# A pruned matmul on one core: the second token pair's load moved from ScalarE's queue to SyncE's

## The chip, the cores and the metric

One NeuronCore of a Trainium2 chip runs the whole program. The time is device microseconds of one execution. Before the change the median of 3 runs is 233.1 us (232.97 to 233.29). The profile is of one execution, which took 233.29 us.

## The reference

A weight matrix `w` (1024 x 1024) is pruned 2:4 along its rows: in each group of 4 neighbouring rows, column by column, the two entries of largest magnitude stay and the others become zero. The pruned matrix is multiplied with 8192 tokens and a bias is added. All arrays are bf16.

```python
B, S, D = 16, 512, 1024
N, M = 2, 4
G = D // M
wg = w.reshape(G, M, D)
mag = jnp.abs(wg)
order = jnp.argsort(mag, 1)
thr = jnp.take_along_axis(mag, order[:, M - N:M - N + 1, :], 1)
mask = (mag >= thr).astype(w.dtype)
wp = (wg * mask).reshape(D, D)
return jnp.einsum("bsd,df->bsf", x, wp) + b
```

## The kernel before

The 8192 tokens are 64 tiles of 128. The contraction of 1024 is 8 slices of 128 rows, and the 1024 output columns are two halves of 512, each with one PSUM bank.

The weights are loaded so that the four rows of a group lie beside each other in one partition (`w_gh`, L60 to L71), which lets VectorE find thresholds without moving data between partitions. They are cut into six pieces (L61): the first row half in four pieces of 256 columns, the second in two of 512. `abs_piece` (L109) and `prep_piece` (L124) compute magnitudes, thresholds, mask and the pruned weights of one piece. Piece 0 is pruned in parts, so that TensorE can begin before the piece is done.

TensorE must not wait for all pieces, so the first 14 tiles are computed in an order written out by hand, the string FRONT (L285 to L299). Tiles 0 to 7 use the first row half in the layout in which it was loaded. Their tokens have to be transposed and regrouped to fit it: token halves are loaded plainly (`load_x`, L76, tiles `xh`), transposed on TensorE with an identity (`transpose_half`, L177; token T of FRONT; matmuls at L182), copied from PSUM to SBUF by ScalarE (`copy_half`, L184; C; L187, tiles `xT`), and used as stationary operand of `mm_part` (L191; N and M; L203). In FRONT, `N.0.1.0` is piece 0, tile 1, row slice 0. A tile's four transposes read one `xh`; its matmuls read its `xT` and a pruned piece. W and w are matmuls of constants (L105) ahead of the first transposes.

The second row half of tiles 0 to 7 comes by a transposing DMA (`xg`, L324), tiles 8 to 13 by two more (`xfill`, L259), and both use `wp_nat`, the pruned weights in natural row order, which DMAs make from the pieces (`unpack`, L170 to L172). From tile 14 on a plain loop (L361 to L377) runs 16 matmuls for each tile on tokens from transposing DMAs (`xTs`, `xTb`, L271); VectorE adds the bias while it empties the banks (L248), and ScalarE's queue sends the outputs.

`K` (L26) keeps each engine's instructions in the order in which they are written. DMAs are issued by SyncE (SP) and ScalarE (ACT), each on a queue of its own; in the profile SP's DMAs are q1 and ScalarE's are q10. At the start, SP issues the first two of the four group rows of piece 0, then the token pair 0 and 1 (`xh_0`), tile 4 (`xh_4`), tile 5 (`xh_5`), piece 1, the pair 6 and 7 (`xh_6`), pieces 2 and 3 in one, and then FRONT's first DMAs: piece 4 and the first transposing load. ScalarE issues the other two group rows of piece 0 and the pair 2 and 3 (`xh_2`), and then loads its function table and makes its first copy (L100). DMAs signal through eight semaphores handed out in turn, so that a later DMA is issued only when the earlier one with its semaphore has landed. In the program before, the first transposing load (L259) has the semaphore that `xh_2` used.

Of the kernel before, what the change touches and what calls it, by code (L numbers as in the profile page):

```python
# [10 lines left out]
def kernel(  # L11
# [7 lines left out]
    nc = tc.nc  # L19
# [56 lines left out]
    def load_x(ta, tb, eng=nc.sync):  # L76
        xt = const.tile([P, tb - ta, KH], bf16, name=f"xh_{ta}")
        src = xf[ta * P:tb * P, 0:KH].rearrange("(t p) c -> p t c", p=P)
        K(eng.dma_start(xt[:], src))
        for t in range(ta, tb):  # L80
            xh[t] = xt[:, t - ta, :]
# [1 line left out]
    load_w(0, 0, 256, nc.sync, 0, 2)  # L83
    load_w(0, 0, 256, nc.scalar, 2, 4)
    load_x(0, 2)
    load_x(2, 4, nc.scalar)
    load_x(4, 5)
    load_x(5, 6)
    load_w(0, 256, 512)
# [316 lines left out]
```

## Time and profile before

| what | value |
|---|---|
| median of 3 runs | 233.1 us |
| profiled execution | 233.29 us |
| its span, first to last instruction | 231.5 us |
| TensorE matmuls busy | 226.3 us (98%) |
| VectorE busy | 120.2 us (52%) |
| ScalarE busy | 18.0 us (8%) |
| granted TensorE clock | 1.000 |
| HBM read, written | 3.41 MB, 16.78 MB |

"Busy" is the time in which an engine ran at least one instruction that counts; PE is TensorE's matmuls, PEld its weight loads, which overlap with matmuls, and DVE is VectorE. The chain that ended last is followed back from the last instruction, at each step to what released it. In a timeline the columns are start, duration, engine, line, operation, output and input, shapes, count, and in brackets the idle time before it and what ended it. DMA issues stand as SPq or ACTq: the duration there is the issue alone, and the landing is listed apart, as microseconds from the start of the issue. A table by stretches of time lists for each the busy time and count of PE, PEld, DVE, ACT and POOL, then the granted clock, the share of the 16 DMA engines' time, and GB/s.

### The profile page before, as it was taken

What the parts mean: (1) busy time and instruction counts of PE and PEld (TensorE: products, weight loads), DVE (VectorE), ACT (ScalarE), POOL (GpSimd) and SP (SyncE); (2) the same over time, 40 slices, a digit from 0 to 9 for tenths busy, and PEclk for the clock granted to TensorE, in tenths of its full rate; (3) what the DMA queues carried; (4) which work ended last, traced back from release to release, by engine and by line L of the source; (5) the groups of instructions that cost most, each with busy time, mean ns of one, the idle gap of its engine ahead of it and who ended that gap; (6) DMA issues with size and microseconds to landing.
All of it is one profiled execution on the core that took longest, in us unless ns stands there. A gap on an engine that the chain in (4) does not pass through costs nothing.

```text
span 231.5 us, 2773 instructions
## 1 busy us (share of the span) xinstructions
PE 226.3 (98%) x1137; PEld 110.5 (48%) x1156; DVE 120.2 (52%) x213; ACT 18.0 (8%) x33; POOL 0.7 (0%) x6
## 2 busy tenths in 40 slices
PE   7999999999999999999999999999999999999995
PEld 3887444444444444444444444444444444444443
DVE  3999887867997324424424424423423433433434
ACT  2867500000000000000000000000000000000000
POOL 1000000000000000000000000000000000000000
PEclk9999999999999999999999999999999999999999
DMA  6999889999647222991249622595128921122222
GB/s 196 295 193 270 192 177 184 267 252 307 258 181 272 91 95 65 233 290 55 84 120 265 159 95 91 131 258 179 69 91 210 316 108 40 53 91 91 91 93 91
DMA packets 77100, 38.19 MB, mean 165 GB/s; under 512 B 63136, under 2 KB 68896, under 8 KB 77088
## 3 DMA queue, kind: packets, MB, share of 16 engines
q1 hardware_dynamic: 67712, 20.91, 42.0%
q10 hardware_dynamic: 9376, 17.11, 20.0%
q8 instruction: 9, 0.15, 0.3%
q14 instruction: 3, 0.02, 0.0%
HBM read 3.41 MB, written 16.78 MB: 87 GB/s over the span
## 4 chain that ended last, share of the span: by engine, by line
PE 96%; DMA 2%; issue 1%; DVE 0%; SPq 0%
PE bank L371 73%; PE bank L203 17%; PE bank L263 6%; DMA xh<-in_x_dram 2%; PE bank L182 1%; DVE o_last L354 0%; SPq L71 0%; PE bank L105 0%
## 5 line engine op out<-in xcount | busy, mean ns | idle before, releaser
L371 PE MATMUL bank<-wp_nat,xTb 128*128 128x512 bf16 x737 | 161.7, 379 | 0.8
L248 DVE TENSOR_TENSOR o_pair<-bank,bias_sb 128x512 bf16<-128x512 f32 x104 | 67.3, 687 | 99.5 <-PE bank L371 94.2
L371 PEld LDWEIGHTS <-xTb 128*128 128x128 bf16 x752 | 73.6, 98 | 88.7
L239 DVE TENSOR_TENSOR stage<-bank,stage 128x512 f32<-128x512 f32 x22 | 14.2, 687 | 4.1 <-PE bank L203 4.1
L203 PE MATMUL bank<-w,xT 128*128 128x256 bf16 x128 | 14.7, 273 | 0.0
L243 DVE TENSOR_TENSOR o_pair<-stage,bias_sb 128x512 bf16<-128x512 f32 x22 | 14.0, 683 | 0.0
L203 PE MATMUL bank<-wp_nat,xg 128*128 128x512 bf16 x62 | 13.9, 379 | 0.1
L203 PEld LDWEIGHTS <-xT 128*128 128x128 bf16 x128 | 12.2, 98 | 1.8 <-ACT xT L187 0.3
L235 ACT COPY stage<-bank 128x512 f32<-128x512 f32 x22 | 11.5, 613 | 4.5 <-PE bank L203 4.5
L203 PE MATMUL bank<-wp_nat,xfill 128*128 128x512 bf16 x47 | 10.6, 379 | 0.1
L263 PE MATMUL bank<-wp_nat,xfill 128*128 128x512 bf16 x47 | 10.5, 379 | 0.1
L203 PEld LDWEIGHTS <-xg 128*128 128x128 bf16 x64 | 6.3, 98 | 7.6
L263 PEld LDWEIGHTS <-xfill 128*128 128x128 bf16 x48 | 4.7, 98 | 5.7
L203 PEld LDWEIGHTS <-xfill 128*128 128x128 bf16 x48 | 4.7, 98 | 5.5
L371 PE MATMUL bank<-wp_nat,xTs 128*128 128x512 bf16 x32 | 7.1, 379 | 0.0
L150 DVE TENSOR_TENSOR mask<-mag,thr 128x512 bf16<-128x512 bf16 (+3 forms) x10 | 5.6, 581 | 0.2
L153 DVE TENSOR_TENSOR w<-w,mask 128x512 bf16<-128x512 bf16 (+3 forms) x10 | 5.6, 580 | 0.1
L371 PEld LDWEIGHTS <-xTs 128*128 128x128 bf16 x32 | 3.1, 98 | 3.8
L105 PE MATMUL bank<-const-bfloat16-1.0 128*128 128x512 bf16 (+1 forms) x12 | 4.0, 493 | 0.8 <-PEq L390 0.8
L187 ACT COPY xT<-bank 128x512 bf16<-128x512 bf16 x8 | 4.1, 605 | 3.0 <-PE bank L182 3.0
L120 DVE TENSOR_SCALAR mag<-w 128x512 uint16<-128x512 uint16 (+2 forms) x6 | 2.7, 466 | 2.8 <-DMA w<-in_w_dram 2.7
L263 PE MATMUL bank<-wp_nat,xTb 128*128 128x64 bf16 (+3 forms) x40 | 3.7, 251 | 0.0
(20 smaller groups left out, 26.1 us busy)
## 6 DMA issues: line engine op xcount, KB each, us to landing
out_dram<-o_pair ACTq DMA_DIRECT2D x24, 512.0 KB, 2.8
out_dram<-o_pair ACTq DMA_DIRECT2D x15, 256.0 KB, 2.0
wp_nat<-w SPq DMA_DIRECT2D x16, 128.0 KB, 2.8
w<-in_w_dram SPq DMA_DIRECT2D x3, 512.0 KB, 5.9
xh<-in_x_dram SPq DMA_DIRECT2D x2, 256.0 KB, 4.2
xh<-in_x_dram ACTq DMA_DIRECT2D x1, 256.0 KB, 4.4
xh<-in_x_dram SPq DMA_DIRECT2D x2, 128.0 KB, 4.2
w<-in_w_dram SPq DMA_DIRECT2D x1, 256.0 KB, 4.5
```

What stands on the lines that cost most here:

```text
L105: K(nc.tensor.matmul(bank[7][:, :n], lhsT=ones[:, :P], rhs=ones[:, :n], start=True, stop=True))
L120: K(nc.vector.tensor_single_scalar(mag[:, ms].bitcast(u16), w_of(i)[:, ms].bitcast(u16), 0x7FFF, op=Alu.bitwise_and))
L150: K(nc.vector.tensor_tensor(mask[:, ms, c], mag[:, ms, c], tb, op=Alu.is_ge))
L153: K(nc.vector.tensor_tensor(w_of(i)[:, ms, c], w_of(i)[:, ms, c], mask[:, ms, c], op=Alu.mult))
L187: K(nc.scalar.copy(xt[:], src))
L203: K(nc.tensor.matmul(dst, lhsT=lhs, rhs=rhs, start=c0 == 0 and m == 0, stop=c1 == FH and m == 3))
L235: K(nc.scalar.copy(stage[(h, t)][:], bank[own[(h, t)]][:]))
L239: K(nc.vector.tensor_tensor(st, bank[own[(2 + h, t)]][:], st, op=Alu.add))
L243: K(nc.vector.tensor_tensor(get_o(t)[:, f], stage.pop((h, t))[:], bias_sb[:, f], op=Alu.add))
L248: K(nc.vector.tensor_tensor(get_o(t)[:, f], bank[bk][:], bias_sb[:, f], op=Alu.add))
L263: K(nc.tensor.matmul(bank[bk][:, :c1 - c0], lhsT=xN[t][:, kt, :], rhs=wp_nat[h][:, kt, c0:c1], start=kt == 0, stop=kt == KT - 1))
L371: K(nc.tensor.matmul(bank[bks[h]][:], lhsT=xN[t][:, kt, :], rhs=wp_nat[h][:, kt, :], start=kt == 0, stop=kt == KT - 1))
```

## The change

```diff
@@ -83,7 +83,7 @@
     load_w(0, 0, 256, nc.sync, 0, 2)
     load_w(0, 0, 256, nc.scalar, 2, 4)
     load_x(0, 2)
-    load_x(2, 4, nc.scalar)
+    load_x(2, 4)
     load_x(4, 5)
     load_x(5, 6)
     load_w(0, 256, 512)
```

`load_x` issues on SyncE where no engine is given. The load of tiles 2 and 3 is therefore issued by SP, as its third DMA, behind tiles 0 and 1 and ahead of tile 4. ScalarE is left with one load at the start, the second two group rows of piece 0. In the built program nothing else moves: TensorE's, VectorE's and GpSimd's instructions are the same, and only the two semaphores of `xh_0` and `xh_2` are exchanged, so that the first transposing load now has the semaphore that `xh_0` used.

## The prediction

> **What bounds the kernel now.** I read the page from the top: busy shares, then the chain that ended last, then the first 11 us instruction by instruction, because every DMA that the change touches is issued before 2 us.
>
> ```profile
> PE 226.3 (98%) x1137; PEld 110.5 (48%) x1156; DVE 120.2 (52%) x213; ACT 18.0 (8%) x33; POOL 0.7 (0%) x6
> ...
> PE 96%; DMA 2%; issue 1%; DVE 0%; SPq 0%
> ```
>
> TensorE is the bound and its work is not touched. The time can only change through where TensorE's stream begins and where it is held. The chain in order of time shows the only part outside TensorE:
>
> ```profile
> 0.73 0.45 SPq L71
> 1.18 0.06 issue
> 1.24 3.96 DMA xh<-in_x_dram
> 5.20 0.05 issue
> 5.24 1.08 PE bank L182 x16
> ```
>
> So the first token pair (xh_0, tokens 0 and 1) lands at 5.20 and starts the transposes T.0. The weight loads of TensorE, which lead its matmuls, show where it is held after that:
>
> ```profile
> 5.24 0.93 PEld L182 LDWEIGHTS <-xh 128*128 128x128 bf16 x16 [0.89 <-DMA xh<-in_x_dram]
> ...
> 6.39 0.15 PEld L203 LDWEIGHTS <-xT 128*128 128x128 bf16 x2
> 6.82 0.11 PEld L203 LDWEIGHTS <-xT 128*128 128x128 bf16 x2 [0.28 <-ACT xT L187]
> 6.94 0.33 PEld L182 LDWEIGHTS <-xh 128*128 128x128 bf16 x4
> 7.31 1.43 PEld L203 LDWEIGHTS <-xT 128*128 128x128 bf16 x14
> ```
>
> The reader is to see two holds. Tile 1's first matmul (6.82) waits for ScalarE's second copy, and tile 2's (7.31) comes when the third copy has ended. The copies run back to back:
>
> ```profile
> 5.69 3.04 ACT L187 COPY xT<-bank 128x512 bf16<-128x512 bf16 x6 [2.41 <-PE bank L182]
> ```
>
> Six copies in 3.04 us are one per 0.49, with 0.60 for the last one (median 597 ns). Copies 1, 2 and 3 end at about 6.28, 6.77 and 7.25; the loads that need the second and third start 0.05 later. The train starts at 5.69 because T.0 does, so both holds descend from xh_0's landing.
>
> **The size of the holds.** Taken one by one in the trace, weight loads stand 0.109 us apart behind a 256-column matmul and 0.056 behind a transpose. From the load at 6.444 the third load on stands at 6.943 and would stand at 6.771 at this spacing: 0.17 lost. From 7.164 the third stands at 7.433 instead of 7.385: 0.05 lost. Together 0.22 us.
>
> **What else is due just in time.** xh_2 (tokens 2 and 3) was issued at 1.25 and landed after 4.4, at 5.62; its first weight load is at 5.66, straight behind T.1. Tile 4 (xh_4) landed at 5.98 and T.4 starts at 6.17. VectorE's second prune of piece 0 ends at 6.36 and the first pruned matmul's load is at 6.39, its start at 6.44. These three end within 0.2 us of TensorE's need, so a later xh_2 moves 6.44 one for one, and an earlier one buys at most 0.03.
>
> **The change part by part.** *ACT queue:* one issue of 0.505 us goes. ScalarE's table load moves from 1.79 to about 1.3. ScalarE next waits for T.0 until 5.69 (2.41 idle), so this is worth 0. Without that cover it would be 0.5.
>
> *SP queue:* xh_2 goes in behind xh_0. Three x issues took 1.44, so a place in the queue is 0.48 to 0.50. Every later SP issue moves by that: xh_4 from 1.75 to 2.24, xh_5 2.25 to 2.74, w piece 1 from 2.72 to 3.2, xh_6 3.44 to 3.9, the two 512 KB w loads (4.09, 4.70) by the same, all of them one DMA each.
>
> *The queue past 5 us:* the xfill transpose starts now at 5.63, because its semaphore is that of xh_2 (5.62) while SP was free at 5.33. After, its semaphore slot belongs to xh_0 and SP is free at 5.33 + 0.49 = 5.82: it starts 0.2 later, its 6.48 us then end at 12.3, and the unpacks (12.25), the last w load (15.79) and xg (16.46) go 0.2 later. The next unpacks at 22.48 wait for VectorE's prune, so the shift ends there. Covers: the unpacked rows landed at 17.85 and are read at 21.2; the xg rows landed at 23.8 and are read at 26.3. Worth 0; uncovered it would be 0.2.
>
> *Landings:* the shift in issue matters only if the engines ran dry. They do not:
>
> ```profile
> 3.25:3.75 0.50, 0.50 (x3) 0.19 (x2) 0.17 (x1) 0.04 (x1) 0.00 (x0) 1.00 1.08 260
> 3.75:5.25 1.50, 0.78 (x6) 0.32 (x4) 1.50 (x9) 0.00 (x0) 0.00 (x0) 1.00 1.02 358
> 5.50:8.50 3.00, 3.00 (x39) 2.57 (x37) 2.81 (x11) 2.81 (x6) 0.00 (x0) 1.00 1.05 330
> ```
>
> The last two columns are DMA share and GB/s. From 3.75 to 5.25, with both rings at work, the engines are full at 358 GB/s, and the packets split 52.7% (SP's ring) to 49.5% (ACT's): the two pairs share the engines. From 5.5 to 8.5 SP's ring alone moved 330.
>
> ```profile
> q1 hardware_dynamic: 297, 0.28, 52.7%
> q10 hardware_dynamic: 271, 0.26, 49.5%
> ```
>
> In one ring xh_0 comes first. It had 0.13 MB by 3.75; the other 0.13 MB at 330 GB/s take 0.4, so its packets end near 4.15 instead of about 4.7, and it lands near 4.7 to 4.8 instead of 5.20. The 0.26 MB of xh_2 follow in 0.8: packets end near 4.95 instead of 5.25, so it lands at 5.3 to 5.6. What comes behind is bounded by the rates: 1.5 us at 330 instead of 358 leave 0.04 MB over, 0.13 us. So xh_4 lands at 5.98 to 6.11 (needed 6.17), w piece 1 at 7.25 to 7.38.
>
> *Piece 1 on VectorE:* its first operation started at 7.27, on the landing, and its first half was pruned at 10.36; TensorE reads that from 10.74. A landing at 7.38 makes it 10.49; TensorE 0.22 earlier asks at 10.52. It holds, barely. Piece 2 (half at 13.68, asked 14.24) has 0.5 to spare.
>
> *Sum:* TensorE's 6.44 stays (gain 0 to 0.03). With xh_0 at 4.78, copies 1 and 2 end at 5.87 and 6.35, before tile 1's load at 6.55; copy 3 ends near 6.84, before tile 2's at 7.22. Both holds go: 0.22. The holds at copies 7 and 8 (near 9.9 and 10.4) repeat, since T.6 and T.7 move with TensorE. The profiled execution took 233.29, of which 231.5 is span; 0.22 off gives 233.07. The median of the runs shown is 0.19 below that execution, so the forecast is 233.1 - 0.2 = 232.9. The bounds on the gain in xh_0's landing are 0 (then nothing) and 0.5; 0.26 is enough.
>
> I count 0.2% (0.47 us) as what a measurement can tell from no change, so this is a gain inside it.
>
> The Trainium skill speaks against any gain: "DMA: Bandwidth & Descriptors", "Issuing engines are not separate DMA queues", says that DMAs of both engines run on the same 16 DMA engines and that issuing on two saves only sequencer time. By that rule the change would cost one SP issue, which is the issue-bound rival below; the trace agrees with the sharing (52.7 to 49.5), and whether order within a ring is worth anything the rule leaves open.
>
> **Rivals.** *Hidden anyway* (0.10): xh_0 does not land earlier, being held by latency, not by its neighbour; xh_2 lands as before. For: 260 GB/s in 3.25 to 3.75 with the ring almost alone. Time 233.1.
>
> *Issue-bound* (0.15): landings stand 4.0 to 4.5 after their issue for all x loads and piece 1, and this may be a fixed delay. Then xh_0 stays at 5.20, xh_2 lands at 6.12, the first pruned matmul's load moves by 0.50 to 6.89; no copy is waited for any more, which gives 0.22 back; piece 1's half at 10.86 comes before TensorE's 11.02. Loss 0.28: 233.4. Against: the full engines above.
>
> *A ring has a rate of its own* (0.20), the one that ends slower: if one ring alone draws only what each drew from 3.75 to 5.25 (0.26 MB in 1.5 us, 180 GB/s), xh_0 gains nothing and xh_2 comes 1.46 after it, at 6.66, 1.04 late. Less the 0.22 that is then no longer waited for, 0.8: 233.9. It decides as soon as xh_2 lands more than 0.22 late, after 5.84, and by over 0.2% after 6.31. For: the slow half microsecond before 3.75. Against: 330 GB/s of that ring alone later.
>
> *More than the holds* (0.10): the two w halves of piece 0 (3.55 and 3.73) land 0.3 earlier too, VectorE starts so much earlier and 6.44 moves with it: 0.22 + 0.3, 232.6. Against: before 3.25 almost no x packet was moving, so there is little to take away.
>
> **How the numbers follow.** Forecast 0.45, the rivals as given. Within 0.2% (232.63 to 233.57) fall forecast, hidden and issue-bound, 0.70, less 0.02 for a forecast that spreads below and 0.03 for an issue-bound case that spreads above: 0.65. Faster is 0.10 + 0.02 = 0.12, slower 0.20 + 0.03 = 0.23. The range 232.5 to 233.9 leaves out the lower part of "more than the holds" and the upper half of the slow ring, some 0.15. The likeliest case's own range is 232.7 to 233.2.
>
> **What would show it.** Right: xh_0's weight load (L182) near 4.8, a wait inside the 16 transposes before T.2, the hold on copy 2 gone from the waits, the first pruned matmul still near 6.4, piece 1's first operation within 0.13 of 7.27, and 0.2 off the span. Wrong: T.0 still at 5.24 (hidden or issue-bound); T.2 at 6.1 (issue-bound) or beyond 6.3 (slow ring); a new wait of TensorE on VectorE near 10.5, if piece 1 is more than 0.15 late.

## The result and the profile after

The changed kernel takes 234.56 us (median of 6 runs, 234.16 to 235.49) against 233.14 before (median of 6): the ratio is 1.0065 with a 95% interval of 1.0051 to 1.0079. It is slower by 1.4 us, outside the range. The profiled execution took 234.63, its span is 232.8 against 231.5.

TensorE's weight loads of the changed kernel show where the 1.3 us of span are lost (columns as in the timeline before):

```profile
4.67 0.78 PEld L182 LDWEIGHTS <-xh 128*128 128x128 bf16 x8
6.48 0.49 PEld L182 LDWEIGHTS <-xh 128*128 128x128 bf16 x8 [1.03 <-DMA xh<-in_x_dram]
...
7.19 0.37 PEld L203 LDWEIGHTS <-xT 128*128 128x128 bf16 x4
7.58 0.33 PEld L182 LDWEIGHTS <-xh 128*128 128x128 bf16 x4
7.85 1.46 PEld L203 LDWEIGHTS <-xT 128*128 128x128 bf16 x14
10.16 0.48 PEld L182 LDWEIGHTS <-xh 128*128 128x128 bf16 x8 [0.84 <-DMA xh<-in_x_dram]
```

T.0 begins at 4.67 instead of 5.24, but T.2 waits for xh_2 until 6.48, so the first pruned matmul's load stands at 7.19 instead of 6.39: 0.80 lost. The holds on copies 2 and 3 are gone (four L203 loads in one piece, no wait inside), and with the next loads TensorE is 0.58 behind: 0.22 came back. Then T.6, which never waited before, waits for xh_6 until 10.16; its load stood at 8.74 before. From there TensorE is 1.34 late and stays so.

The transfers themselves, by stretches of time, first of the kernel before:

```profile
3.75:4.25 0.50, 0.50 (x4) 0.21 (x3) 0.50 (x4) 0.00 (x0) 0.00 (x0) 1.00 0.89 317
4.25:4.75 0.50, 0.28 (x3) 0.10 (x1) 0.50 (x4) 0.00 (x0) 0.00 (x0) 1.00 1.10 383
...
7.50:9.00 1.50, 1.50 (x17) 1.37 (x16) 1.43 (x6) 1.23 (x3) 0.00 (x0) 1.00 1.04 348
```

and of the changed one:

```profile
3.75:4.25 0.50, 0.50 (x3) 0.23 (x2) 0.50 (x4) 0.00 (x0) 0.00 (x0) 1.00 0.93 104
4.25:4.75 0.50, 0.50 (x4) 0.22 (x3) 0.50 (x3) 0.00 (x0) 0.00 (x0) 1.00 0.25 86
...
7.50:9.00 1.50, 1.50 (x19) 1.37 (x16) 0.08 (x1) 1.50 (x4) 0.00 (x0) 1.00 0.71 151
```

The last column is GB/s. Two holes have opened. After xh_0 is through, the engines move 104 and 86 GB/s where they moved 317 and 383; and from 7.5 to 9 they move 151 where they moved 348. The DMA share beside them (0.93 and 0.25) books a packet's whole time where it starts, so it does not show how full each half microsecond was.

Last landings of the first x and w loads, read from the trace's landing events (us), for the two profiled executions and three further ones:

| load | before | before, 2nd | after | after, 2nd | after, 3rd |
|---|---|---|---|---|---|
| xh_0 | 5.20 | 4.82 | 4.38 | 4.75 | 4.58 |
| xh_2 | 5.62 | 5.17 | 6.44 | 6.01 | 6.10 |
| xh_4 | 5.98 | 5.58 | 6.76 | 6.38 | 6.46 |
| piece 1 | 7.25 | 6.84 | 8.89 | 7.50 | 7.55 |
| xh_6 | 7.94 | 8.34 | 10.12 | 11.00 | 9.09 |
| time of that execution | 233.29 | 232.97 | 234.63 | 235.51 | 233.62 |

### The profile page after: what moved, and what is told of

Its sections match the earlier page's. It is cut to its first block, busy times and chain, and to the rows that moved or that the text cites. A ratio compares the mean times of both kernels' runs of the same rounds, so it can differ in the third digit from the quotient of the medians.

```text
span 232.8 us, 2792 instructions
## 1 busy us (share of the span) xinstructions
PE 227.9 (98%) x1156; PEld 110.9 (48%) x1156; DVE 120.2 (52%) x213; ACT 18.2 (8%) x33; POOL 0.7 (0%) x6
## 3 DMA queue, kind: packets, MB, share of 16 engines
HBM read 3.41 MB, written 16.78 MB: 87 GB/s over the span
## 4 chain that ended last, share of the span: by engine, by line
PE 94%; DMA 3%; SPq 1%; DVE 0%; issue 0%
PE bank L371 73%; PE bank L203 16%; PE bank L263 6%; DMA xh<-in_x_dram 3%; SPq L79 1%; SPq L71 0%; DVE o_last L354 0%; PE bank L182 0%
## 5 line engine op out<-in xcount | busy, mean ns | idle before, releaser
L248 DVE TENSOR_TENSOR o_pair<-bank,bias_sb 128x512 bf16<-128x512 f32 x104 | 67.3, 687 | 99.5 <-PE bank L371 96.3
L203 PE MATMUL bank<-w,xT 128*128 128x256 bf16 x128 | 14.5, 273 | 0.0
L203 PE MATMUL bank<-wp_nat,xg 128*128 128x512 bf16 x64 | 14.1, 379 | 0.0
L203 PEld LDWEIGHTS <-xT 128*128 128x128 bf16 x128 | 12.3, 98 | 1.6
L203 PE MATMUL bank<-wp_nat,xfill 128*128 128x512 bf16 x48 | 10.7, 379 | 0.0
L203 PEld LDWEIGHTS <-xg 128*128 128x128 bf16 x64 | 6.2, 98 | 7.6
L203 PEld LDWEIGHTS <-xfill 128*128 128x128 bf16 x48 | 4.7, 98 | 5.5
L182 PE MATMUL bank<-ident,xh 128*128 128x128 bf16 x32 | 2.8, 233 | 1.4 <-DMA xh<-in_x_dram 1.4
```

Of the source, the lines that this page charges most:

```text
L182: K(nc.tensor.transpose(dst[:, m, :], xv[:, m, :], ident[:]))
L203: K(nc.tensor.matmul(dst, lhsT=lhs, rhs=rhs, start=c0 == 0 and m == 0, stop=c1 == FH and m == 3))
L248: K(nc.vector.tensor_tensor(get_o(t)[:, f], bank[bk][:], bias_sb[:, f], op=Alu.add))
```

## The experiments

**Again, for the landings alone.** Both kernels once more, the changed one twice.

> The changed kernel once more, for its landings alone. Theory 'stall' (with the two pairs in one line the packets of the second stand still at part of the DMA engines, in each execution): xh_0 lands before 4.7, xh_2 after 6.0 with more than 0.9 between its first and last engine, xh_6 after 8.8. Theory 'chance' (the profiled execution was an unlucky one): xh_2 lands before 5.8 and xh_6 before 8.4.

> As the run beside it: stall: xh_2 after 6.0, xh_6 after 8.8; chance: xh_2 before 5.8, xh_6 before 8.4.

> The kernel before once more, for its landings: stall: xh_0 5.2, xh_2 5.6, piece 1 7.25, xh_6 7.9, each within 0.4. Chance: one of them is more than 0.8 later.

The table has the landings. xh_2 is always after 6.0, with 1.2 to 1.4 between its first and last engine (0.4 to 0.5 before), and xh_6 always after 9: not chance. What varies is the depth: 211 and 256, then 287 and 270 GB/s in the two half microseconds instead of 104 and 86. The time goes with xh_6: 9.09 gives 233.62, 10.12 gives 234.63, 11.00 gives 235.51. T.6 in the second and the third execution of the changed kernel, and in the second of the kernel before:

```profile
11.04 0.48 PEld L182 LDWEIGHTS <-xh 128*128 128x128 bf16 x8 [2.16 <-DMA xh<-in_x_dram]
9.13 0.48 PEld L182 LDWEIGHTS <-xh 128*128 128x128 bf16 x8 [0.16 <-DMA xh<-in_x_dram]
8.42 0.56 PEld L182 LDWEIGHTS <-xh 128*128 128x128 bf16 x8
```

In the kernel before, xh_6 cost nothing, but the margin is not always wide: it landed at 7.94 for a load at 8.74, and in the second execution at 8.34 for a load at 8.42. That execution also landed xh_2, piece 1 and xh_6 0.41 to 0.44 away from the expected times, a little more than the 0.4 allowed.

**The lag alone.** The kernel before, with a tiny load in the place where the change puts xh_2:

```diff
     load_x(2, 4, nc.scalar)
+    lag = const.tile([P, 8], bf16, name="lag")
+    K(nc.sync.dma_start(lag[:], xf[0:P, 0:8]))
     load_x(4, 5)
```

> The kernel before, with a tiny load (128 x 16 bytes into a tile nobody reads) put on SP's queue in the place where the change puts xh_2; xh_2 stays on ScalarE's queue. SP's later issues move by one place as in the change, the bytes do not. Theory 'lag' (SP's later loads land late because they are issued a place later): xh_6 lands near 10, piece 1 near 8.9, time near 234.5. Theory 'ring' (loads that follow each other on one queue with the other one empty stall at the DMA engines) and theory 'order' (the second pair is late because the first takes the engines before it): landings within 0.5 of before (xh_6 7.9 to 8.4, piece 1 7.25 to 7.75), 233.1 to 233.4.

Measured 233.85, ratio 1.0032 (1.0021 to 1.0044). Half of each theory: xh_0, xh_2, xh_4 and piece 1 land at 4.66, 5.11, 5.55 and 7.25, none later than before, and there is no first hole (375 and 332 GB/s, with xh_2 on the other queue). But xh_6, issued at 3.92 instead of 3.44, lands at 8.91, and T.6 waits for it 0.67:

```profile
8.95 0.48 PEld L184 LDWEIGHTS <-xh 128*128 128x128 bf16 x8 [0.67 <-DMA xh<-in_x_dram]
```

That is the only wait of TensorE in this execution (233.49) that the kernel before does not have. So one load more in SP's queue, with next to no bytes, makes about half of the loss, and the profile puts it on xh_6.

**No second load.** The changed kernel with the two pairs in one load:

```diff
-    load_x(0, 2)
-    load_x(2, 4)
+    load_x(0, 4)
```

> The changed kernel with the two pairs loaded by one DMA of 512 KB on SP's queue in place of two of 256 KB. Theory 'boundary' (the engines stand still where the second load follows the first): one load has no such place, all four tiles land near 5.3, T.0 starts there, 233.2 to 234.0 with xh_6 still late. Rival 'volume' (the standstill comes at a time or after so many bytes, whatever the loads): it lands at 6.0 or later with a spread over 0.9, 234.5 or more.

Measured 233.55, ratio 1.0011 (0.9999 to 1.0023). Same bytes, same queue, nothing on ScalarE's: the four tiles land at 5.32 with 0.6 between the engines, and the hole is not there.

```profile
3.75:4.25 0.50, 0.50 (x3) 0.22 (x2) 0.50 (x4) 0.00 (x0) 0.00 (x0) 1.00 1.08 385
4.25:4.75 0.50, 0.50 (x4) 0.19 (x2) 0.50 (x3) 0.00 (x0) 0.00 (x0) 1.00 1.10 357
```

SP's queue alone sustains 357 to 385 GB/s here. So a ring has no lower rate of its own; the hole belongs to the step from one load to the next. SP's queue is also as long as before in this kernel (xh_6 issued at 3.48, landed at 8.80, due 8.95): the hole and the wait for xh_6 are gone at once.

**Which step.** A single tile put between the pairs (SP: xh_0, xh_4, xh_2, xh_5):

```diff
     load_x(0, 2)
-    load_x(2, 4)
     load_x(4, 5)
+    load_x(2, 4)
```

> The changed kernel with xh_4 (one tile, 128 KB) put between the two pairs on SP's queue: xh_0, xh_4, xh_2, xh_5. As many issues as in the changed kernel. Theory 'pair behind pair' (the engines stand still where a pair load follows a pair load directly): xh_4 and xh_2 land in step, near 5.2 and 5.9, each with its engines within 0.6; piece 1 near 7.3; only the later xh_6 costs; 233.6 to 234.0. Theory 'third load' (whatever is third on a queue that early waits): xh_4 already lands after 5.9 with more than 0.9 between its engines, xh_2 after 6.4; 234.4 or more.

Measured 234.64, ratio 1.0054 (1.0037 to 1.0072); the seven runs lie between 233.90 and 234.87. In the profiled one, which took 233.91:

```profile
3.75:4.25 0.50, 0.50 (x5) 0.25 (x3) 0.50 (x4) 0.00 (x0) 0.00 (x0) 1.00 0.40 45
4.25:4.75 0.50, 0.50 (x11) 0.48 (x8) 0.50 (x3) 0.04 (x1) 0.00 (x0) 1.00 0.68 176
```

The hole is as deep with a load of 128 KB behind xh_0 as with one of 256 KB, so it does not need a pair behind a pair. The landings are nearer to that theory all the same: the engines stay in step (0.5 between first and last), xh_4 lands at 5.43, xh_2 at 6.16, piece 1 at 7.48, and xh_6 at 9.39 makes T.6 wait for 0.40. Neither theory is whole: third load has the hole behind xh_0, but not the spread and not landings after 5.9 and 6.4.

Both halves of piece 0 on ScalarE's queue, which makes the pairs first and second on SP's:

```diff
-    load_w(0, 0, 256, nc.sync, 0, 2)
+    load_w(0, 0, 256, nc.scalar, 0, 2)
     load_w(0, 0, 256, nc.scalar, 2, 4)
```

> The changed kernel with the first half of piece 0 moved to ScalarE's queue as well, so that xh_0 and xh_2 are the first and second load of SP's queue, and SP's queue is as long as before. Pair behind pair: xh_2 still has more than 0.9 between its engines and lands a second or more behind xh_0, near 6. Third load: xh_2 is the second and lands before 5.4 with its engines within 0.7, and what is third (xh_4) is late instead, after 6.2. The w halves may land up to 0.4 later, which VectorE would hand on; time 233.4 to 234.6.

Measured 235.08, ratio 1.0092 (1.0058 to 1.0126), for a reason of its own: the w halves share the engines with the pairs and land at 4.62 and 5.79, so VectorE starts late. The question is answered by the stretch, which has no hole:

```profile
3.75:4.25 0.50, 0.50 (x3) 0.22 (x2) 0.00 (x0) 0.00 (x0) 0.00 (x0) 1.00 1.12 371
4.25:4.75 0.50, 0.50 (x8) 0.39 (x7) 0.10 (x1) 0.00 (x0) 0.00 (x0) 1.00 1.11 371
```

xh_2 lands at 5.58. With the pair behind a pair as first and second load there is no hole; where there is one, it lies before the third load of SP's queue. Whether the place or the moment counts is not separated: the third load is issued at 1.74 to 1.76 in every run, and here it is due only after 4.75. (xh_4, third here, lands at 6.17 with 0.73 between its engines, just short of the 6.2 expected; xh_2 has 0.94 while the w half is beside it, so the spread alone proves nothing.)

Tiles 4 and 5 in one load, with xh_2 on ScalarE's queue as before:

```diff
     load_x(2, 4, nc.scalar)
-    load_x(4, 5)
-    load_x(5, 6)
+    load_x(4, 6)
```

> The kernel before with tiles 4 and 5 loaded by one DMA of 256 KB in place of two of 128 KB: SP's queue is a place shorter, and a pair now follows the pair xh_0 on it, with xh_2 beside them on the other queue. Pair behind pair: the load of tiles 4 and 5 has more than 0.9 between its engines and lands after 6.5; 233.5 to 234. Third load: the same. If the stand-still needs the other queue to be empty: it lands near 6.3 with its engines within 0.7, piece 1 and xh_6 up to 0.4 earlier than before, 232.9 to 233.2.

Measured 233.49, ratio 1.0009 (1.0000 to 1.0018). From 3.75 to 4.75 the engines move 381 and 309 GB/s, since xh_2 is there; the dip comes after it (235 from 4.75 to 5.25). Tiles 4 and 5 land at 6.44 with 0.95 between engines: the pair on the other queue covers the hole, it does not remove it. xh_6, issued at 2.97, lands at 8.01.

**The other arrangements.** Exchanging the pairs between the queues:

```diff
-    load_x(0, 2)
-    load_x(2, 4, nc.scalar)
+    load_x(0, 2, nc.scalar)
+    load_x(2, 4)
```

> The kernel before with the two pairs exchanged between the queues: xh_0 on ScalarE's, xh_2 on SP's. Both queues carry what they carried before. Ring and lag: piece 1 and xh_6 land as before (7.25 and 7.9, within 0.3), xh_0 lands near 5.6 where xh_2 did, T.0 starts 0.4 later: 233.1 to 233.6. Order: the same. If SP's queue is bad for xh_2 whatever else is queued, xh_2 lands after 6 here too and the time is above 234.

233.63, ratio 1.0026 (1.0006 to 1.0046): xh_0 lands at 5.38, T.0 starts at 5.42, piece 1 (7.03) and xh_6 (7.70) are no later than before. Both pairs on ScalarE's queue:

```diff
-    load_x(0, 2)
+    load_x(0, 2, nc.scalar)
     load_x(2, 4, nc.scalar)
```

> Both token pairs on ScalarE's queue, xh_0 before xh_2; SP's queue is one load shorter than before. Ring: two queues are at work again, so piece 1 and xh_6 land as before or up to 0.5 earlier (6.8 to 7.3 and 7.4 to 7.9); xh_2, behind a pair on its queue, may still be late (5.6 to 6.4); time 233.1 to 233.9, below the changed kernel. Lag: all of SP's loads land 0.5 earlier, time 232.9. Order: xh_2 lands near 6.4 as in the changed kernel, xh_0 near 4.4, time near 233.7.

234.43, ratio 1.0065 (1.0040 to 1.0090): xh_0 at 5.73 and xh_2 at 6.84; no theory had xh_0 late. Tile 5, now third on SP's queue, has the hole: from 3.5 to 4.25 that queue moves next to nothing. The other order in SP's line, xh_2 first:

```diff
-    load_x(0, 2)
     load_x(2, 4)
+    load_x(0, 2)
```

> The changed kernel with the two pairs in the other order in SP's line: xh_2 first, xh_0 behind it. Theory 'line' (the second of two pairs in one line is late, whichever it is): xh_2 lands before 4.8 with its engines within 0.6, xh_0 after 6.0 with more than 0.9 between first and last engine; T.0 starts after 6.0 and copies 2 and 3 hold TensorE again; 234.4 to 235.4. Rival 'address' (the rows of xh_2 are slow to read alone): xh_2 in front has the wide spread and lands after 5.3.

237.25, ratio 1.0143 (1.0082 to 1.0205, of four runs from 234.85 to 238.21): xh_2 lands at 4.64 and xh_0 at 7.06 with 2.3 between its engines. The late one is the later one, not the rows of xh_2; the time is worse than the theory's, since T.0 waits for it.

**Moving xh_6.** To ScalarE's queue at once, in the changed kernel; in the kernel before; and behind ScalarE's first copy, in each of the two:

```diff
-    load_x(6, 8)
+    load_x(6, 8, nc.scalar)
```

> The changed kernel with the pair of tiles 6 and 7 (xh_6) moved to ScalarE's queue, so that SP keeps xh_0 and xh_2 in one line and the other queue has a pair again. Ring: the stalls shrink with two queues at work; xh_6 lands before 7, xh_2 near 5.6 to 6.0, the wait before T.6 is gone, time 232.9 to 233.5. Lag: piece 1 stays at about 8.9 and only the wait for xh_6 (0.8) goes, 233.7. Order: xh_2 stays at 6.4, 233.7.

> The kernel before with the pair xh_6 also on ScalarE's queue, behind xh_2; SP's queue is one load shorter than before, and two short of the changed kernel. Theory 'lag' (half of the loss is that SP's later loads come a place later, xh_6 last of them): piece 1 lands up to 0.4 earlier, xh_6 before 7, no wait ahead of T.6, 232.8 to 233.2. Theory 'stall by pairs in one line': xh_6 is the second pair on ScalarE's queue and stalls, which does no harm since it is due at 8.7, but the engines are held for others: xh_4 or piece 1 land later than before by 0.5, 233.3 to 234.

> The changed kernel with the load of tiles 6 and 7 (xh_6) taken off SP's queue and issued by ScalarE behind its first copy, near 2.8; SP keeps xh_0 and xh_2 in one line. Theory 'xh_6' (the larger part of the loss is TensorE's wait ahead of T.6 for the last load of that queue): xh_6 lands before 8.5 and that wait is gone, while xh_2 still lands at 6.0 to 6.4; time 233.3 to 233.7. Theory 'xh_2' (the loss is made by the late second pair): the time stays at 234.3 or above.

> The kernel before with xh_6 issued by ScalarE near 3.2, behind its first copy. Theory 'xh_6': in the kernel before TensorE does not wait for xh_6, so nothing is to be won there: 232.9 to 233.2, xh_6 landing before 7.5, piece 1 within 0.4 of 7.25. If any load more on ScalarE's queue disturbs the first ones (as in the run with it issued at 1.8), xh_4 or piece 1 is over 0.5 late and the time above 233.6.

Measured ratios 1.0057 (1.0028 to 1.0086), 1.0035 (1.0021 to 1.0049), 1.0051 (1.0024 to 1.0077) and 1.0026 (1.0008 to 1.0044). The wait ahead of T.6 is gone in all four, and none is faster than before: a 256 KB load more on ScalarE's queue takes the engines while xh_2 (first and third kernel) or xh_4 and xh_5 (second and fourth) are due. The issue meant for 2.8 went out at 1.32 and 1.85, ahead of the copies at 2.55 and 3.08 that precede it in the program: in these two traces ScalarE did not hold the DMA back for a copy that still waited, so the two kernels do not test a late issue. In the third kernel xh_2 landed at 7.29, 2.5 behind xh_0.

**Fewer, larger loads.** Tiles 0 to 3 in one load on ScalarE's queue, and tiles 0 to 3 and 4 to 5 in one load each on SP's:

```diff
-    load_x(0, 2)
-    load_x(2, 4, nc.scalar)
+    load_x(0, 4, nc.scalar)
```

> The kernel before with tiles 0 to 3 loaded by one DMA of 512 KB on ScalarE's queue, SP's queue one place shorter than before: no pair follows a pair, and piece 1 and xh_6 are issued 0.5 earlier than before. All theories: the four tiles land near 5.4 to 5.8, piece 1 before 7, xh_6 before 7.6. If the later T.0 (0.2 to 0.5) is not made up, 233.3 to 233.7; if the shorter queue pays, 232.8 to 233.1.

```diff
-    load_x(0, 2)
-    load_x(2, 4)
-    load_x(4, 5)
-    load_x(5, 6)
+    load_x(0, 4)
+    load_x(4, 6)
```

> The changed kernel with tiles 0 to 3 in one load of 512 KB and tiles 4 and 5 in one of 256 KB, all on SP's queue, which is then one place shorter than before and two shorter than the changed kernel. Theory 'hole' (the third load of SP's queue does not move before 4.5, and in the kernel before xh_2 on the other queue covers this): the third load is due only near 5, so no hole; tiles 0 to 3 land near 5.3, tiles 4 and 5 near 6.1, piece 1 before 7, xh_6 before 8.5; 233.1 to 233.6. Rival 'pair behind a bigger load stands still too': tiles 4 and 5 after 6.8 with more than 0.9 between their engines, 233.8 or more.

The first took 235.02, ratio 1.0078 (1.0047 to 1.0109): it shares the engines with SP's loads and lands at 6.26, later than all theories had it. The second took 233.71, ratio 1.0018 (1.0007 to 1.0029), between the two theories: no hole before 4.75, four tiles at 5.49, xh_6 at 8.64; but tiles 4 and 5 land at 6.84 with 1.4 between engines, as the rival had it, and T.4 waits. No version beat the kernel before.

## Why the prediction was wrong

**The step that failed** is "Landings: the shift in issue matters only if the engines ran dry. They do not.", and with it the term that rests on it: the 0.26 MB of xh_2 were to follow xh_0 at 330 GB/s in 0.8. In the changed kernel the engines moved 104 and 86 GB/s there, and xh_2 landed at 6.44 instead of 5.3 to 5.6. The averages used (358 GB/s over 1.5 us, 330 over 3 us) are right for their stretches, but hide that SP's queue hardly moves in the kernel before too, for about a quarter of a microsecond. Its DMA view from 4.50 to 4.75 (share of the 16 engines' time in the last column):

```profile
q10 hardware_dynamic: 87, 0.09, 96.3%
q1 hardware_dynamic: 17, 0.01, 14.9%
```

SP's queue (q1) is at 14.9% between xh_0 and xh_4, and nothing is lost because xh_2 on ScalarE's queue has the engines for 96.3%. The second execution of before shows the same from 3.75 to 4.25, with 27.5% beside 80.3%. The change took xh_2 away from there and put it behind the hole. The same stretch of the changed kernel, 4.50 to 4.75, with 123 GB/s in all instead of 389:

```profile
q1 hardware_dynamic: 34, 0.03, 35.3%
```

The prediction costed the move as more bytes in one line, and lost what the second queue was worth: cover while SP's queue waits for its third load. That SP's queue has little to move there, and is not only kept off by xh_2, is inferred from the changed kernel, whose engines stay slow at the same moment with xh_2 gone from beside it.

**xh_6 was never costed.** The prediction listed its issue moving from 3.44 to 3.9 and stopped there; its landing and due time (7.94 against 8.74, 0.8 to spare) were not worked out, though it was the last landing before a long stretch of TensorE. Over all runs with xh_6 on SP's queue it lands at 7.70 to 8.80 if issued by 3.5 (nine executions) and at 8.91 to 11.00 if issued at 3.92 or later (six). TensorE waited for it 0.84, 2.16 and 0.16 in the three executions of the changed kernel. What the late xh_2 had cost by then, at the first of the fourteen L203 loads, was 0.54, 0.11 and 0.20 against the first execution of the kernel before, and 0.36 more against its second. So which term is larger changes from one execution to the next; in the lag run xh_6 is the only new wait.

**Right were** the place on ScalarE's queue (worth 0; its first copy came at 5.43); the shift of each SP issue by 0.5 (piece 1 at 3.23, xh_6 at 3.95); that xh_0 lands earlier (4.38, 4.75, 4.58; forecast 4.7 to 4.8), though the second execution of the kernel before, at 4.82, shows that 5.20 was a late one; that both holds go and give back 0.22; and that the later transposing load costs nothing, although its issue took 7.99 us instead of 6.48, so that what SP issues behind it came 1.6 to 1.8 later and not 0.2. Piece 1 landed 1.64 late instead of at most 0.13, and its first half was pruned at 12.00, just ahead of TensorE's load for it at 12.09. Without the wait for xh_6 that load would have stood at 10.74 + 0.58 = 11.32, and TensorE would have been held here instead, for nearly as long.

**The rivals.** The issue-bound rival had xh_2 nearly right (6.12; measured 6.44, 6.01, 6.10) for a delay from issue that xh_0 does not have (3.1 us instead of 4.0), and missed xh_6 like the forecast. "A ring has a rate of its own" had the side right, and its mechanism falls with the one-load kernel: 357 to 385 GB/s on SP's queue alone. "Hidden anyway" and "more than the holds" fall with xh_0 at 4.38 and piece 0 within 0.1 of before.

The Trainium skill's rule in "DMA: Bandwidth & Descriptors", "Issuing engines are not separate DMA queues", that issuing on two engines saves only sequencer time, is half borne out: in the lag run one issue more, 0.46 us of SP, cost 0.3% (0.76 us). The rest is not in it: here the second queue also covered a hole in the first.

**What stays open** is what happens inside the hole. The third load of SP's queue, issued near 1.75, moves little before 4.25 to 4.75 in nearly all runs, whatever its size; in the profiled execution of the changed kernel single packets of 1.0 to 1.3 us stand there where the others take 0.046, and the depth differs from one execution to the next. Counted over the time that they take, packets occupy 0.57 of the engines' time from 3.75 to 4.75, of which 0.32 is in packets of over 0.2 us: part of the engines stand and part have nothing to do. Whether descriptors or data are late the traces do not show.

Open, too, is what makes xh_6 so late. In the profiled execution of the changed kernel packets of 0.8 to 1.3 us stand again from 7.65 on, and in the second execution of the kernel before the engines fall to 227 and 203 GB/s in the two half microseconds from 6.5 as well. An earlier issue alone does not help: in the four kernels that issue xh_6 at 2.93 to 3.00 it lands at 8.01 to 8.64, no sooner than in those that issue it at 3.44 or 3.48.

## What to carry to other kernels

An average rate over a stretch does not show that a queue keeps the engines fed: look at each queue in quarter microseconds, and ask what the other queue is covering before taking a load off it. For every issue that a change moves, write down its landing and its due time, down to the last one in the queue. Where two loads had to share a queue, one load of 512 KB in place of the two pairs kept both the place in the queue and the rate here; joining tiles 4 and 5 as well won nothing.

## What the runs showed of the hardware

A wait early in the kernel can cost more than itself. In the profiled execution of the third of the xh_6 kernels TensorE stood for 2.06 us until xh_2 landed at 7.29, and then ran at a lower granted clock (third column from the right: 0.63 and 0.61, 1.00 before and after):

```profile
5.00:7.30 2.30, 0.42 (x8) 0.26 (x5) 2.09 (x10) 1.07 (x2) 0.00 (x0) 1.00 0.98 307
7.30:9.40 2.10, 2.07 (x20) 1.83 (x21) 0.41 (x1) 1.56 (x3) 0.00 (x0) 0.63 1.10 363
9.40:11.80 2.40, 2.40 (x17) 1.86 (x15) 2.30 (x9) 0.59 (x1) 0.00 (x0) 0.61 1.24 195
11.80:13.50 1.70, 1.70 (x22) 1.42 (x21) 1.67 (x6) 1.15 (x3) 0.00 (x0) 1.00 1.28 290
```

Fourteen weight loads of L203 took 2.36 us there and 1.46 in the changed kernel. That execution took 236.36, while the median of its kernel is 234.12. The trace's clock events give one stretch of 3.41 us at half rate. Of the ten runs of this kernel, two show a mean clock of 0.993, and they took 236.36 and 235.94; the other eight, at 0.999 or 1.000, took 233.84 to 234.54.

The first of the xh_6 kernels shows the same: its profile has a wait of 1.65 for xh_2 and then 3.41 us at half rate from 6.99, and its two runs at 0.993 took 235.75 and 236.44, the other six 233.64 to 234.28. The length of the wait does not decide it alone. In the second execution of the changed kernel TensorE waited 2.16 ahead of T.6, and in the kernel with both halves of piece 0 on ScalarE's queue 1.94 ahead of its second L203 load, and behind both the weight loads went at their usual pace (fourteen in 1.46 in the latter).
